# Second MLP of a fused attention kernel: other pairs of block products per PSUM bank, all engines in written order, part of the x work on GpSimd

## The chip, the cores and the metric

One core of a Trainium2 chip runs the whole program. The metric is the device time of one execution in microseconds (us). The engines are TensorE (PE, with its weight loads as PEld), VectorE (DVE), ScalarE (ACT), GpSimd (POOL) and SyncE (SP, which issues all DMAs of this kernel).

## The reference

Attention with keys and values averaged over 8 positions, then two MLPs, all in float32. Only the last function matters here; x has 4608 rows of 512 and comes from the first MLP.

```python
def _moe2_ref(x, w1, w2, w3, w_out) -> np.ndarray:
    a = x @ w1                       # 512 -> 1024
    b = x @ w2
    h = a * b @ w3                   # 1024 -> 1024
    return (h @ w_out).astype(np.float32)
```

## The kernel before

The first part (attention and first MLP) writes x, transposed, to a scratch tensor `x2d` in DRAM as nine groups `j` of 512 rows, each in four blocks of 128x512 words. Then `wf = w3 @ w_out` is made once. The second MLP is the rest of the program, and the change lies in it alone.

Each matrix that TensorE multiplies is split in two numbers, a high part (`h`, ScalarE copy that rounds) and a low part (`l`, VectorE subtract); a product of two such matrices takes three matmuls (high times high, high times low, low times high).

**One unit.** A unit is `ab(j, fc)`: group `j` (9 of them), column chunk `fc` of 128 hidden units (8 of them), 72 units in all. The two products x@w1 and x@w2 of the unit come from seven block products, p1 to p7, each of sums of blocks of x (`xs`, seven split blocks `th`/`tl`) and sums of blocks of the weights. Each block product is 6 matmuls of 256 columns (L869 to L871). They are issued in the order p1, p6, p5, p2, p7, p4, p3 into PSUM banks of tag `pr` (4 buffers, two halves of 256 columns each): p1 and p2 share a bank, p6 and p7, p5 and p3; p4 has one alone. What comes out of PSUM: ScalarE copies p1 (L873); VectorE makes `u2` = p1+p6 (L875), `a` parts (L877, L879, L887) and `b` parts (L881, L882, L884); GpSimd multiplies the halves of `a` and `b` (L885, L888). The product `a` is split into `ph` (ScalarE, L98) and `pl` (VectorE, L99).

**The output product.** `finish` of a unit is 12 matmuls of 512 columns (`out_fc`, L901, L903, L904: eight with `ph`, then four with `pl`; in the last unit of a group three for each of the four accumulators in turn). It is issued one unit later, between p4 and p3 of the next unit (`pend`). After a group's last unit, `evac` scales the four accumulators into `ot` tiles (2 buffers; L910 on VectorE, L912 on ScalarE) and SP stores them. The ninth group's store has the shape [2, 64, 512] on the DRAM side, the others 128 rows.

**The next group's x.** `Blocks.load` (written after the unit fc=2) loads four blocks to `xq` tiles and makes four sums on VectorE (L836, L837, L839, L840); `Blocks.split` splits a block on ScalarE and VectorE. There are 9 buffers for `th` and 9 for `tl`; seven are in use, so two blocks are split early and the other five in unit fc=7, after each product that frees a slot.

**Order.** TensorE's order is as written. The other engines' orders in this phase are the scheduler's.

Of the kernel before, what the change touches and what calls it, by code (L numbers as in the profile page):

```python
# [8 lines left out]
F32 = mybir.dt.float32  # L9
F32R = mybir.dt.float32r  # L10
I32 = mybir.dt.int32
U32 = mybir.dt.uint32
AF = mybir.ActivationFunctionType
ALU = mybir.AluOpType
# [4 lines left out]
def attention_moe_kernel(  # L19
# [25 lines left out]
    nc = tc.nc  # L45

    B, H, S, D = q.shape
    P = 128
    C = H * D
    NP = H // 2  # L50
    F = w_in.shape[1]
    FC = F // P
# [7 lines left out]
    U = 256  # L60
# [12 lines left out]
    def bank(name):  # L73
        return PS.tile([P, 512], F32, tag="ba", name=name, bufs=3)
# [22 lines left out]
    def split(hi, lo, src):  # L97
        nc.scalar.activation(hi, src, AF.Copy)  # L98
        nc.vector.tensor_tensor(lo, src, hi.bitcast(F32), ALU.subtract)  # L99
# [49 lines left out]
    class Rounded:  # L149
        def __init__(self, w, i):  # L150
            self.w, self.i = w, i

        def load(self):
            self.t = self.words()
            nc.sync.dma_start(self.t.rearrange("p n t -> p (n t)"), piece(self.w.bitcast(I32), self.i, 1024))
# [529 lines left out]
    M2 = R = o2 = None  # L685
# [23 lines left out]
    with tc.manual_schedule(engines={mybir.EngineType.PE, mybir.EngineType.SP}):  # L709
        for s_ in range(min(events), SLOTS * (NU + 1) + 2):  # L710
# [4 lines left out]
            kind, n = HEAVY[c], c % 4  # L715
# [16 lines left out]
    def bankp(name):  # L732
        return PB.tile([P, 2, U], F32, tag="pr", name=name, bufs=4)
# [9 lines left out]
    PRODUCTS = (  # L743
        ("p1", [t[:, 0:2] for t in w1p]),
        ("p6", s2),
        ("p5", s1),
        ("p2", [t[:, 2:4] for t in w1p]),
        ("p7", s3),
        ("p4", w2b),
        ("p3", s4),  # L750
    )
# [31 lines left out]
    def w3_T(m):  # L783
        th = R.tile([P, FC, P], F32R, tag="w3h", name=f"w3h{m}", bufs=2)
        tl = R.tile([P, FC, P], F32R, tag="w3l", name=f"w3l{m}", bufs=2)
        for i in range(2):
            t = R.tile([P, 512], F32, tag="stg", name="stg", bufs=4)
            nc.sync.dma_start(t, piece(f32w["w3f"], 2 * m + i))
            pw = bank(f"pw{m}_{i}")
            for c in range(4):  # L790
                nc.tensor.transpose(pw[:, c * P : c * P + P], t[:, c * P : c * P + P], ident)
            split(th[:, 4 * i : 4 * i + 4], tl[:, 4 * i : 4 * i + 4], pw.rearrange("p (c n) -> p c n", c=4))
        return th, tl
# [12 lines left out]
    nxt = w3_T(0)  # L806
    for m in range(FC):
        cur = nxt
        if m + 1 < FC:
            nxt = w3_T(m + 1)  # L810
        wf_rows(m, cur)
        if m in BLOCKS_AT:
            i = BLOCKS_AT.index(m)
# [4 lines left out]
    M2 = ctx.enter_context(tc.tile_pool(name="mlpb", bufs=2, reuse_waits="tile"))  # L818

    class Blocks:  # L820


        def __init__(self, j):
            self.j, self.ready = j, []

        def load(self):
            def raw(r, h):
                t = M2.tile([P, 2, U], F32, tag="xq", name=f"xq{self.j}", bufs=7)
                if r is not None:
                    nc.sync.dma_start(t, x2d[self.j, h, r])  # L830
                return t

            b11, b12, b22, b21 = raw(0, 0), raw(0, 1), raw(1, 1), raw(1, 0)
            t1, t2, t4 = raw(None, 0), raw(None, 0), raw(None, 0)
            tt = nc.vector.tensor_tensor
            tt(t1, b12, b11, ALU.subtract)  # L836
            tt(t2, b22, t1, ALU.subtract)  # L837
            t3 = b12
            tt(t3, b22, b12, ALU.subtract)  # L839
            tt(t4, b21, t2, ALU.subtract)  # L840
            self.todo = [b11, t2, t1, b21, t3, t4, b22]

        def split(self, n=1):
            for src in self.todo[:n]:
                h = M2.tile([P, 2, U], F32R, tag="th", name=f"th{self.j}", bufs=SLOT2)
                l = M2.tile([P, 2, U], F32R, tag="tl", name=f"tl{self.j}", bufs=SLOT2)
                split(h, l, src)
                self.ready.append((h, l))
            del self.todo[:n]

    def ab(j, fc, xs, nxt):
        fsl = slice(fc * P, fc * P + P)
        nm = f"{j}_{fc}"
        tt = nc.vector.tensor_tensor
        p1, u2 = [M2.tile([P, U], F32, tag=t, name=t + nm, bufs=1) for t in ("p1", "u2")]

        a, b = [M2.tile([P, 2, U], F32, tag=t, name=t + nm) for t in ("a", "b")]
        r, pair = {}, {}
        for ((name, (wh, wl)), (th, tl)) in zip(PRODUCTS, xs.ready):
            if name == "p3" and pend is not None:  # L860
                finish(*pend)

            if name in ("p1", "p6", "p5", "p4"):
                pair[name] = bankp(name + nm)
                o = r[name] = pair[name][:, 0]
            else:
                o = pair[{"p2": "p1", "p7": "p6", "p3": "p5"}[name]][:, 1]
            for c in range(2):
                nc.tensor.matmul(o, wh[:, c, fsl], th[:, c], start=c == 0, stop=False)  # L869
                nc.tensor.matmul(o, wh[:, c, fsl], tl[:, c], start=False, stop=False)  # L870
                nc.tensor.matmul(o, wl[:, c, fsl], th[:, c], start=False, stop=c == 1)  # L871
            if name == "p1":
                nc.scalar.activation(p1, o, AF.Copy)  # L873
            elif name == "p6":
                tt(u2, p1, o, ALU.add)  # L875
            elif name == "p5":
                tt(a[:, 1], u2, o, ALU.add)  # L877
            elif name == "p2":
                tt(a[:, 0], p1, o, ALU.add)  # L879
            elif name == "p7":  # L880
                tt(b[:, 0], u2, o, ALU.add)  # L881
                tt(b[:, 1], b[:, 0], r["p5"], ALU.add)  # L882
            elif name == "p4":
                tt(b[:, 0], b[:, 0], o, ALU.add)  # L884
                nc.gpsimd.tensor_tensor(a[:, 0], a[:, 0], b[:, 0], ALU.mult)  # L885
            elif name == "p3":
                tt(a[:, 1], a[:, 1], o, ALU.add)  # L887
                nc.gpsimd.tensor_tensor(a[:, 1], a[:, 1], b[:, 1], ALU.mult)  # L888
            if fc == FC - 1 and nxt is not None:
                nxt.split()  # L890
        ph = M2.tile([P, 512], F32R, tag="ph", name="ph" + nm, bufs=3)
        pl = M2.tile([P, 512], F32R, tag="pl", name="pl" + nm, bufs=3)
        split(ph, pl, a.rearrange("p a n -> p (a n)"))
        return ph, pl

    def out_fc(fc, pp, t, lo):
        ph, pl = pp
        wh, wl = wf[0][:, fc], wf[1][:, fc]
        ts = slice(t * P, t * P + P)
        if lo:  # L900
            nc.tensor.matmul(accs[t], pl[:, ts], wh, start=False, stop=(fc == FC - 1))  # L901
        else:
            nc.tensor.matmul(accs[t], ph[:, ts], wh, start=(fc == 0), stop=False)  # L903
            nc.tensor.matmul(accs[t], ph[:, ts], wl, start=False, stop=False)  # L904

    def evac(j, t):
        ot = M2.tile([P, C], F32, tag="ot", name=f"ot{j}_{t}", bufs=2)
        k = kap[:, 4 * j + t : 4 * j + t + 1]
        if t % 2 == 0:
            nc.vector.tensor_scalar(ot, accs[t], k, None, ALU.mult)  # L910
        else:
            nc.scalar.activation(ot, accs[t], AF.Copy, scale=k)  # L912
        if j == B:
            to = out.rearrange("(b s) c -> b s c", s=S)[2 * t : 2 * t + 2, 512:S, :]
        else:
            to = out[S * j : S * j + 512, :].rearrange("(p t) c -> p t c", t=4)[:, t]
        nc.sync.dma_start(to, ot)

    accs = None

    def finish(j, fc, pp):

        nonlocal accs
        if fc == 0:
            accs = [bank(f"acc{j}_{t}") for t in range(4)]
        if fc < FC - 1:
            for t in range(4):
                out_fc(fc, pp, t, False)
            for t in range(4):
                out_fc(fc, pp, t, True)  # L930
        else:
            for t in range(4):
                out_fc(fc, pp, t, False)
                out_fc(fc, pp, t, True)
                evac(j, t)


    SLOT2 = 9
    pend = None
    xs = Blocks(0)  # L940
    xs.load()
    xs.split(7)
    with tc.manual_schedule(engines={mybir.EngineType.PE}):
        for j in range(NB):
            nxt = Blocks(j + 1) if j + 1 < NB else None
            for fc in range(FC):
                pp = ab(j, fc, xs, nxt)
                pend = (j, fc, pp)
                if fc == 2 and nxt is not None:
                    nxt.load()  # L950
                    nxt.split(SLOT2 - 7)
            xs = nxt
        finish(*pend)


_INS = ['q', 'k', 'v', 'moe_w_in', 'moe_w_out', 'moe_g_ln', 'moe2_w1', 'moe2_w2', 'moe2_w3', 'moe2_w_out']
# [26 lines left out]
```

## Time and profile before

| | us |
|---|---|
| median of 3 runs | 1355.95 (1352.96 to 1356.12) |
| profiled execution, its own time | 1354.67 |
| profiled execution, span | 1352.9 |
| TensorE matmul busy | 1228.2 (91% of the span) |
| VectorE busy | 857.6 (63%) |
| ScalarE busy | 529.6 (39%) |
| GpSimd busy | 352.9 (26%) |

The span is the time from the first to the last instruction. Line numbers are those of the kernel before. Names in the rows drop trailing numbers: `p` is a bank of a block product or the copy of p1, `u` is `u2`; `w1h`, `s2h`, `s1h`, `s3h`, `w2bh` and `s4h` are weights of p1 and p2, p6, p5, p7, p4 and p3. Matmuls are pipelined, so the start of a matmul to the start of the next, not its duration, is its cost. L99 is the line of the helper `split` for all low parts, L98 that for all high parts.

### The profile page before, as it was taken

The page shows a single profiled execution, that of the slowest core. Times are in us where ns is not written, and L with a number is a line of the kernel's source. Part 1 is how long each engine was busy: PE and PEld are TensorE (multiplying, and loading weights), DVE is VectorE, ACT ScalarE, POOL GpSimd, SP SyncE. Part 2 cuts the span into 40 slices and gives each one's busy share as a digit, 9 for nine tenths or more (in the row PEclk, how much of TensorE's full clock was granted, in tenths as well). Part 3 has the DMA queues.
Part 4 walks back from the last instruction along what each step waited for, and adds up shares of the span by engine and source line. Part 5 has one row for each costly group of instructions (what it writes and reads, how often), then busy time and mean ns, then how long its engine had stood idle before and what let it go on. Part 6 is the DMA issues. An engine that isn't in the chain of part 4 may idle for free.

```text
span 1352.9 us, 21592 instructions
## 1 busy us (share of the span) xinstructions
PE 1228.2 (91%) x8120; PEld 1119.2 (83%) x8120; DVE 857.6 (63%) x1710; ACT 529.6 (39%) x1507; POOL 352.9 (26%) x447
## 2 busy tenths in 40 slices
PE   2467998999999999999999899999999999999992
PEld 2356888888888888899988798999989898989992
DVE  7999777777777777655356646556564646464541
ACT  3355656566666656555353221212121212121210
POOL 4453435253434334220000112111211112111110
PEclk9989999999999999999999899999999999999996
DMA  9433445454535364333042201010100102010000
GB/s 227 116 97 102 133 125 156 117 157 119 141 120 137 102 164 117 98 97 107 26 137 72 71 14 51 16 47 17 47 32 32 56 8 63 1 47 1 32 1 31
DMA packets 85696, 109.41 MB, mean 81 GB/s; under 512 B 43608, under 2 KB 43608, under 8 KB 85592
## 3 DMA queue, kind: packets, MB, share of 16 engines
q1 hardware_dynamic: 85592, 108.03, 28.0%
q8 instruction: 64, 1.05, 0.3%
q14 instruction: 40, 0.33, 0.1%
HBM read 78.65 MB, written 29.36 MB: 80 GB/s over the span
## 4 chain that ended last, share of the span: by engine, by line
PE 65%; DVE 16%; DMA 7%; issue 4%; ACT 3%; POOL 3%; SPq 0%; POOLq 0%; ACTq 0%; DVEq 0%
PE h L539 9%; PE p L869 7%; PE p L870 7%; PE p L871 7%; DMA f<-in_moe_w_dram 5%; PE acc L903 4%; PE acc L904 4%; PE acc L901 4%; PE x L597 4%; PE x L596 4%; PE x L598 4%; PE av L511 2%; PE sc L408 2%; PE lt L582 1%; DVE cvm L180 1%
## 5 line engine op out<-in xcount | busy, mean ns | idle before, releaser
L873 ACT ACTIVATE p<-p 128x256 f32<-128x256 f32 x72 | 27.9, 387 | 408.9 <-PE p L871 408.9
L885 POOL TENSOR_TENSOR a<-a,b 128x256 f32<-128x256 f32 x72 | 55.3, 768 | 445.2 <-DVE b L884 445.2
L596 PE MATMUL x<-lnh,gwh 128*128 128x256 f32 x576 | 166.6, 289 | 0.0
L597 PE MATMUL x<-lnl,gwh 128*128 128x256 f32 x576 | 163.0, 283 | 1.6 <-DVE lnl L586 1.6
L598 PE MATMUL x<-lnh,gwl 128*128 128x256 f32 x576 | 162.8, 283 | 0.0
L887 DVE TENSOR_TENSOR a<-a,p 128x256 f32<-128x256 f32 x72 | 30.3, 421 | 164.0 <-PE p L871 163.1
L188 POOL TENSOR_TENSOR cvb<-cvb,cvm 128x512 f32<-128x512 f32 x47 | 61.9, 1316 | 209.1 <-DVE cvm L180 148.0
L903 PE MATMUL acc<-wfh,ph 128*128 128x512 f32 x288 | 113.4, 394 | 2.0 <-ACT ph L98 2.0
L904 PE MATMUL acc<-wfl,ph 128*128 128x512 f32 x288 | 113.5, 394 | 0.0
L429 ACT ACTIVATE ea<-sc,mx 128x72 f32<-128x72 f32 x320 | 98.4, 328 | 36.6 <-DVE mx L426 36.6
L597 PEld LDWEIGHTS x<-lnl,gwh 128*128 128x128 f32 x576 | 110.0, 191 | 3.0 <-DVE lnl L586 2.2
L596 PEld LDWEIGHTS x<-lnh,gwh 128*128 128x128 f32 x576 | 109.9, 191 | 1.3 <-ACT lnh L585 0.2
L598 PEld LDWEIGHTS x<-lnh,gwl 128*128 128x128 f32 x576 | 109.9, 191 | 0.0
L539 PE MATMUL h<-winh,xh 128*128 128x512 f32 x288 | 101.3, 434 | 0.0
L888 POOL TENSOR_TENSOR a<-a,b 128x256 f32<-128x256 f32 x72 | 56.5, 785 | 141.1 <-DVE a L887 141.1
L539 PE MATMUL h<-winl,xh 128*128 128x512 f32 x288 | 92.3, 403 | 0.0
L539 PE MATMUL h<-winh,xl 128*128 128x512 f32 x288 | 91.1, 398 | 0.0
L586 DVE TENSOR_TENSOR lnl<-lt,lnh 128x512 fp32r<-128x512 f32 x72 | 49.3, 687 | 54.0 <-ACT lnh L585 53.5
L869 PE MATMUL p<-th,w1h 128*128 128x256 f32 x288 | 81.9, 284 | 1.2 <-ACT th L98 1.2
L870 PE MATMUL p<-tl,w1h 128*128 128x256 f32 x288 | 81.9, 284 | 0.4 <-DVE tl L99 0.4
L901 PE MATMUL acc<-wfh,pl 128*128 128x512 f32 x288 | 82.1, 392 | 0.0
L871 PE MATMUL p<-th,w1l 128*128 128x256 f32 x288 | 81.7, 284 | 0.0
(187 smaller groups left out, 3670.0 us busy)
## 6 DMA issues: line engine op xcount, KB each, us to landing
f<-in_moe_w_dram SPq DMA_DIRECT2D x32, 512.0 KB, 6.3
x2d<-xo SPq DMA_DIRECT2D x36, 256.0 KB, 3.0
xq<-x2d SPq DMA_DIRECT2D x36, 256.0 KB, 2.7
out_dram<-ot SPq DMA_DIRECT2D x36, 256.0 KB, 2.3
kv<-in_k_dram SPq DMA_DIRECT2D x32, 256.0 KB, 3.7
q<-in_q_dram SPq DMA_DIRECT2D x32, 256.0 KB, 7.4
kv<-in_v_dram SPq DMA_DIRECT2D x32, 256.0 KB, 3.8
f<-in_moe_w_out_dram SPq DMA_DIRECT2D x16, 512.0 KB, 6.8
```

What stands on the lines that cost most here:

```text
L188: self.engine.tensor_tensor(self.f, self.f, self.m.bitcast(F32), ALU.add)
L429: nc.scalar.activation(e[0:n, x], half[a][:, h], AF.Exp, bias=mx[0:n, x : x + 1], scale=1.0, accum_out=sm[0:n, x : x + 1],)
L539: nc.tensor.matmul(self.ph[:, a], s_[:, c], w_[:, c, a * 512 : a * 512 + 512], start=first, stop=last)
L596: nc.tensor.matmul(o, gw[0][:, f, ws], self.th[:, f], start=(f == 0), stop=False)
L597: nc.tensor.matmul(o, gw[0][:, f, ws], self.tl[:, f], start=False, stop=False)
L598: nc.tensor.matmul(o, gw[1][:, f, ws], self.th[:, f], start=False, stop=(f == FC - 1))
L869: nc.tensor.matmul(o, wh[:, c, fsl], th[:, c], start=c == 0, stop=False)
L870: nc.tensor.matmul(o, wh[:, c, fsl], tl[:, c], start=False, stop=False)
L871: nc.tensor.matmul(o, wl[:, c, fsl], th[:, c], start=False, stop=c == 1)
L901: nc.tensor.matmul(accs[t], pl[:, ts], wh, start=False, stop=(fc == FC - 1))
L903: nc.tensor.matmul(accs[t], ph[:, ts], wh, start=(fc == 0), stop=False)
L904: nc.tensor.matmul(accs[t], ph[:, ts], wl, start=False, stop=False)
```

## The change

In the second MLP:

- p7 gets a bank of its own, which it shares with p4; p6 has its bank alone.
- `finish` is issued before p4 instead of before p3; in the last unit of the last group it is issued after p3.
- `ph` and `pl` of a unit are made inside the next unit: `ph` on ScalarE after the copy of p1, `pl` on VectorE after the p2 addition.
- For all groups but the first, the four sums of x and the low parts of the blocks 0, 1, 3 and 5 are made on GpSimd.
- The next group's loads are written after unit fc=1, two sums after fc=3, two after fc=4, two splits after fc=5, and five splits inside unit fc=7 at the places of the table `LAST`.
- The two parts of a split block lie in one tile (`th`, 9 buffers of two parts); `ph` and `pl` have 2 buffers instead of 3; `ot` has 4 instead of 2.
- All five engines run in the written order in this phase.

```diff
@@ -821,7 +821,7 @@
 
 
         def __init__(self, j):
-            self.j, self.ready = j, []
+            self.j, self.ready, self.n = j, [], 0
 
         def load(self):
             def raw(r, h):
@@ -832,21 +832,32 @@
 
             b11, b12, b22, b21 = raw(0, 0), raw(0, 1), raw(1, 1), raw(1, 0)
             t1, t2, t4 = raw(None, 0), raw(None, 0), raw(None, 0)
-            tt = nc.vector.tensor_tensor
-            tt(t1, b12, b11, ALU.subtract)
-            tt(t2, b22, t1, ALU.subtract)
-            t3 = b12
-            tt(t3, b22, b12, ALU.subtract)
-            tt(t4, b21, t2, ALU.subtract)
-            self.todo = [b11, t2, t1, b21, t3, t4, b22]
-
-        def split(self, n=1):
-            for src in self.todo[:n]:
-                h = M2.tile([P, 2, U], F32R, tag="th", name=f"th{self.j}", bufs=SLOT2)
-                l = M2.tile([P, 2, U], F32R, tag="tl", name=f"tl{self.j}", bufs=SLOT2)
-                split(h, l, src)
-                self.ready.append((h, l))
-            del self.todo[:n]
+            self.todo = [b11, t2, t1, b21, b12, t4, b22]
+
+        def sum(self, o, x, y):
+            (nc.gpsimd if self.j else nc.vector).tensor_tensor(o, x, y, ALU.subtract)
+
+        def sums12(self):
+            b11, t2, t1, b21, b12, t4, b22 = self.todo
+            self.sum(t1, b12, b11)
+            self.sum(t2, b22, t1)
+
+        def sums34(self):
+            b11, t2, t1, b21, b12, t4, b22 = self.todo
+            self.sum(b12, b22, b12)
+            self.sum(t4, b21, t2)
+
+        def hi(self):
+            src = self.todo[len(self.ready)]
+            t = M2.tile([P, 2, 2, U], F32R, tag="th", name=f"th{self.j}", bufs=SLOT2)
+            nc.scalar.activation(t[:, 0], src, AF.Copy)
+            self.ready.append((t[:, 0], t[:, 1]))
+
+        def lo(self):
+            i, self.n = self.n, self.n + 1
+            h, l = self.ready[i]
+            eng = nc.gpsimd if self.j and i in (0, 1, 3, 5) else nc.vector
+            eng.tensor_tensor(l, self.todo[i], h.bitcast(F32), ALU.subtract)
 
     def ab(j, fc, xs, nxt):
         fsl = slice(fc * P, fc * P + P)
@@ -857,26 +868,30 @@
         a, b = [M2.tile([P, 2, U], F32, tag=t, name=t + nm) for t in ("a", "b")]
         r, pair = {}, {}
         for ((name, (wh, wl)), (th, tl)) in zip(PRODUCTS, xs.ready):
-            if name == "p3" and pend is not None:
-                finish(*pend)
-
-            if name in ("p1", "p6", "p5", "p4"):
+            if name == "p4" and pend is not None and (j, fc) != (B, FC - 1):
+                finish()
+
+            if name in ("p1", "p6", "p5", "p7"):
                 pair[name] = bankp(name + nm)
                 o = r[name] = pair[name][:, 0]
             else:
-                o = pair[{"p2": "p1", "p7": "p6", "p3": "p5"}[name]][:, 1]
+                o = pair[{"p2": "p1", "p4": "p7", "p3": "p5"}[name]][:, 1]
             for c in range(2):
                 nc.tensor.matmul(o, wh[:, c, fsl], th[:, c], start=c == 0, stop=False)
                 nc.tensor.matmul(o, wh[:, c, fsl], tl[:, c], start=False, stop=False)
                 nc.tensor.matmul(o, wl[:, c, fsl], th[:, c], start=False, stop=c == 1)
             if name == "p1":
                 nc.scalar.activation(p1, o, AF.Copy)
+                if pend is not None:
+                    pend[2].hi()
             elif name == "p6":
                 tt(u2, p1, o, ALU.add)
             elif name == "p5":
                 tt(a[:, 1], u2, o, ALU.add)
             elif name == "p2":
                 tt(a[:, 0], p1, o, ALU.add)
+                if pend is not None:
+                    pend[2].lo()
             elif name == "p7":
                 tt(b[:, 0], u2, o, ALU.add)
                 tt(b[:, 1], b[:, 0], r["p5"], ALU.add)
@@ -887,14 +902,24 @@
                 tt(a[:, 1], a[:, 1], o, ALU.add)
                 nc.gpsimd.tensor_tensor(a[:, 1], a[:, 1], b[:, 1], ALU.mult)
             if fc == FC - 1 and nxt is not None:
-                nxt.split()
-        ph = M2.tile([P, 512], F32R, tag="ph", name="ph" + nm, bufs=3)
-        pl = M2.tile([P, 512], F32R, tag="pl", name="pl" + nm, bufs=3)
-        split(ph, pl, a.rearrange("p a n -> p (a n)"))
-        return ph, pl
+                for step in LAST[name]:
+                    getattr(nxt, step)()
+        return Product(a.rearrange("p a n -> p (a n)"), nm)
+
+    class Product:
+        def __init__(self, a, nm):
+            self.a, self.nm = a, nm
+
+        def hi(self):
+            self.h = M2.tile([P, 512], F32R, tag="ph", name="ph" + self.nm)
+            nc.scalar.activation(self.h, self.a, AF.Copy)
+
+        def lo(self):
+            self.l = M2.tile([P, 512], F32R, tag="pl", name="pl" + self.nm)
+            nc.vector.tensor_tensor(self.l, self.a, self.h.bitcast(F32), ALU.subtract)
 
     def out_fc(fc, pp, t, lo):
-        ph, pl = pp
+        ph, pl = pp.h, pp.l
         wh, wl = wf[0][:, fc], wf[1][:, fc]
         ts = slice(t * P, t * P + P)
         if lo:
@@ -904,7 +929,7 @@
             nc.tensor.matmul(accs[t], ph[:, ts], wl, start=False, stop=False)
 
     def evac(j, t):
-        ot = M2.tile([P, C], F32, tag="ot", name=f"ot{j}_{t}", bufs=2)
+        ot = M2.tile([P, C], F32, tag="ot", name=f"ot{j}_{t}", bufs=4)
         k = kap[:, 4 * j + t : 4 * j + t + 1]
         if t % 2 == 0:
             nc.vector.tensor_scalar(ot, accs[t], k, None, ALU.mult)
@@ -918,9 +943,10 @@
 
     accs = None
 
-    def finish(j, fc, pp):
+    def finish():
 
         nonlocal accs
+        j, fc, pp = pend
         if fc == 0:
             accs = [bank(f"acc{j}_{t}") for t in range(4)]
         if fc < FC - 1:
@@ -937,20 +963,34 @@
 
     SLOT2 = 9
     pend = None
+
+    LAST = dict(
+        p1=("hi",), p6=("hi",), p5=("lo", "lo", "hi"), p2=("hi",), p7=("lo", "lo", "hi", "lo"), p4=(), p3=()
+    )
+
+    EARLY = {1: ("load",), 3: ("sums12",), 4: ("sums34",), 5: ("hi", "hi", "lo", "lo")}
     xs = Blocks(0)
     xs.load()
-    xs.split(7)
-    with tc.manual_schedule(engines={mybir.EngineType.PE}):
+    xs.sums12()
+    xs.sums34()
+    for _ in PRODUCTS:
+        xs.hi()
+        xs.lo()
+    E = mybir.EngineType
+    with tc.manual_schedule(engines={E.PE, E.SP, E.Activation, E.DVE, E.Pool}):
         for j in range(NB):
             nxt = Blocks(j + 1) if j + 1 < NB else None
             for fc in range(FC):
                 pp = ab(j, fc, xs, nxt)
+                if (j, fc) == (B, FC - 1):
+                    finish()
                 pend = (j, fc, pp)
-                if fc == 2 and nxt is not None:
-                    nxt.load()
-                    nxt.split(SLOT2 - 7)
+                for step in EARLY.get(fc, ()) if nxt is not None else ():
+                    getattr(nxt, step)()
             xs = nxt
-        finish(*pend)
+        pp.hi()
+        pp.lo()
+        finish()
 
 
 _INS = ['q', 'k', 'v', 'moe_w_in', 'moe_w_out', 'moe_g_ln', 'moe2_w1', 'moe2_w2', 'moe2_w3', 'moe2_w_out']
```

## Rows read from the trace of the kernel before

**Rows 1.** Busy us (count) of PE, PEld, DVE, ACT, POOL; clock, DMA share, GB/s.
```profile
766.00:1320.00 554.00, 546.88 (x3765) 507.48 (x3764) 303.70 (x655) 109.77 (x210) 107.39 (x139) 1.00 0.08 29
```

**Rows 2.** ScalarE timeline, copies of p1: start, duration, operation, [idle before <-releaser].
```profile
767.86 0.39 ACT L873 ACTIVATE p<-p 128x256 f32<-128x256 f32 x1 [7.08 <-PE p L871]
...
806.76 0.39 ACT L873 ACTIVATE p<-p 128x256 f32<-128x256 f32 x1 [6.65 <-PE p L871]
...
814.79 0.39 ACT L873 ACTIVATE p<-p 128x256 f32<-128x256 f32 x1 [3.77 <-PE p L871]
...
823.66 0.39 ACT L873 ACTIVATE p<-p 128x256 f32<-128x256 f32 x1 [2.15 <-PE p L871]
...
831.87 0.39 ACT L873 ACTIVATE p<-p 128x256 f32<-128x256 f32 x1 [6.50 <-PE p L871]
...
1317.32 0.39 ACT L873 ACTIVATE p<-p 128x256 f32<-128x256 f32 x1 [6.65 <-PE p L871]
```

**Rows 3.** TensorE timeline, one unit inside a group and the start of the next.
```profile
1174.24 0.28 PE L869 MATMUL p<-th,w1h 128*128 128x256 f32 x1
...
1177.12 0.28 PE L869 MATMUL p<-th,s3h 128*128 128x256 f32 x1
...
1178.56 0.40 PE L903 MATMUL acc<-wfh,ph 128*128 128x512 f32 x1
...
1181.31 0.28 PE L869 MATMUL p<-th,s4h 128*128 128x256 f32 x1
...
1182.02 0.28 PE L869 MATMUL p<-th,w1h 128*128 128x256 f32 x1
```

**Rows 4.** Timeline of all engines in the same unit.
```profile
1175.71 0.63 ACT L98 ACTIVATE ph<-a 128x512 fp32r<-128x512 f32 x1
...
1177.32 0.42 DVE L879 TENSOR_TENSOR a<-p,p 128x256 f32<-128x256 f32 x1
```

**Rows 5.** Timeline of all engines, first unit of the second group.
```profile
814.03 0.74 POOL L885 TENSOR_TENSOR a<-a,b 128x256 f32<-128x256 f32 x1 [6.80 <-DVE b L884]
...
814.36 0.95 DVE L837 TENSOR_TENSOR xq<-xq,xq 128x512 f32<-128x512 f32 x1
...
814.73 1.19 POOL L888 TENSOR_TENSOR a<-a,b 128x256 f32<-128x256 f32 x1
...
815.24 1.22 DVE L839 TENSOR_TENSOR xq<-xq,xq 128x512 f32<-128x512 f32 x1
...
816.61 0.69 DVE L99 TENSOR_TENSOR pl<-a,ph 128x512 fp32r<-128x512 f32 x1 [0.15 <-ACT ph L98]
...
817.69 0.39 PE L869 MATMUL p<-th,s3h 128*128 128x256 f32 x1 [0.83 <-DVE u L875]
```

**Rows 6.** Instruction groups: low parts, and sums on GpSimd elsewhere.
```profile
L99 DVE TENSOR_TENSOR tl<-xq,th 128x512 fp32r<-128x512 f32 x54 | 36.4, 686 | 0.0
...
L188 POOL TENSOR_TENSOR cvb<-cvb,cvm 128x512 f32<-128x512 f32 x47 | 61.9, 1316 | 209.1 <-DVE cvm L180 148.0 <-DVE sm L444 53.7 <-DVE sm L445 4.1
```

**Rows 7.** TensorE timeline, first two units of the phase.
```profile
757.33 0.36 PE L869 MATMUL p<-th,s4h 128*128 128x256 f32 x1 [1.37 <-DVE b L882]
...
761.90 0.39 PE L869 MATMUL p<-th,s3h 128*128 128x256 f32 x1 [0.74 <-DVE u L875]
```

**Rows 8.** Timeline of all engines after the last block product.
```profile
1324.01 0.28 PE L871 MATMUL p<-th,s4l 128*128 128x256 f32 x1
...
1326.27 0.50 PE L903 MATMUL acc<-wfh,ph 128*128 128x512 f32 x1 [1.98 <-ACT ph L98]
...
1328.31 1.35 SPq L917 DMA_DIRECT2D out_dram<-ot  x2
...
1336.62 0.75 DVE L910 TENSOR_SCALAR ot<-acc,kap 128x512 f32<-128x512 f32 x1 [8.34 <-DMA out_dram<-ot]
```

**Rows 9.** Busy by stretch (columns as in group 1), the last stores.
```profile
1329.50:1333.00 3.50, 1.42 (x4) 0.60 (x2) 0.00 (x0) 0.00 (x0) 0.00 (x0) 0.75 0.13 29
1333.00:1351.50 18.50, 0.00 (x0) 0.00 (x0) 0.75 (x1) 0.69 (x1) 0.00 (x0) 0.55 0.13 51
```

## Prediction

> **What bounds the kernel now.** I read the views from the whole to the single wait. The second MLP is the last 600 us of the span, and the change is confined to it. From the third unit to the last, TensorE is busy 546.88 of 554 us at a granted clock of 1.00 (2.4 GHz), while VectorE has 303.70, ScalarE 109.77 and GpSimd 107.39 [rows 1]: the phase is TensorE's, and no edit of the change takes a matmul away. So I first need TensorE's pace without waits. The timeline of one unit inside a group gives it [rows 3]: p1 starts at 1174.24, p7 at 1177.12 (2.88 later), the output product at 1178.56 (4.32), p3 at 1181.31 (7.07), the next p1 at 1182.02. A unit is 7.78 us, an output product 2.75, a block product 0.72, one of the 12 wide matmuls 2.75 / 12 = 0.229. The work is issued back to back; such a unit has nothing to gain.
>
> What is above that floor shows in the starts of the p1 copies, one per unit [rows 2]. From the third unit (767.86) to the 72nd (1317.32) there are 69 units: 549.46 us, where 69 x 7.78 = 536.8. The excess is 12.6. It sits at the group changes: 806.76 to 814.79 is 8.03, to 823.66 is 8.87, to 831.87 is 8.21, that is 0.25 + 1.09 + 0.43 = 1.77 over three units. Seven such changes are 12.4, and the eighth, after which no group is prepared, has the first 0.25: together 12.6, so this is all of it.
>
> The reason is in the timeline there [rows 5]: the first matmul of p7 waited for u2 (0.83 idle). p7 is written to the bank that holds p6, and u2, which reads p6, stood on VectorE behind two sums of 0.95 and 1.22 us and a `pl` of 0.69. Two more places are above the floor: the start of the phase, where p3 waited 1.37 for b and the next unit's p7 0.74 for u2 [rows 7], and the end, where the last output product waited 1.98 for `ph` [rows 8] before four stores follow.
>
> **The change part by part.** Times are counted from a unit's first matmul.
>
> *Banks and order.* p7 no longer shares with p6, so its wait for u2 is gone. The new pairs: p4 goes into p7's bank, and the 2.75 us of the output product stand between them; p3 goes into p5's bank 4.9 us later; p1 and p2 are as before. The output product now starts at 3.60 instead of 4.32. It needs `ph`, which ended 1175.71 + 0.63 = 2.10 into the unit [rows 4]: 1.5 to spare. Its first matmul with `pl` is at 3.60 + 8 x 0.229 = 5.43; `pl` now stands behind the p2 addition, which starts at 3.08 [rows 4], so it ends at 3.08 + 0.42 + 0.69 = 4.2: 1.2 to spare. An ordinary unit costs 7.78 as before.
>
> *Work that moves.* Per group, four sums and four low parts leave VectorE, 8 x 0.69 = 5.5 us [rows 6], for GpSimd, where the nearest row, a 128x512 addition in the first part, has 1316 ns: 8 x 1.32 = 10.5 us. GpSimd has two products of 0.74 per unit [rows 5], so it has room. Sums and the first low parts stand after units 3, 4 and 5, two at a time, 2.6 us behind the product that ends about 1.5 into the next unit; they are over at 4.1 and the next p4 product comes after 6.35. Nothing is queued behind them that is due earlier, and their results are due three to four units later. The loads are written one unit earlier, behind the four stores of the last group on SP, and have over 15 us until the sums: nothing.
>
> *Unit 7 of a group.* ScalarE has p1's copy, `ph` to 2.10, then five high parts of at most 0.63, each after the product that frees its slot; the last is done by 5.3, and the next copy is due after 8. VectorE has seven additions of 0.42 and four low parts (one is `pl`) of 0.69, 5.7 of 7.78 us, without sums. The 0.25 of p3's wait should go. Two tight places stay. `pl` here follows a low part and the p2 addition (3.8) and meets GpSimd's two low parts, the first of which starts when the second high part is done, at about 3.4. Rows 5 show what such a meeting costs: the sum of two SBUF tiles issued at 814.36 took 0.95 where 0.69 is normal [rows 6], the next one 1.22, and GpSimd's product between them 1.19 instead of 0.74; the operations took turns. So `pl` waits for one GpSimd operation, 3.4 + 1.3 = 4.7, and ends near 5.35, just before 5.43. Bounds: `pl` at 4.5 without a meeting, or at 6.65 if both GpSimd operations go first, which holds TensorE for 1.2.
>
> The Trainium skill, SBUF — State Buffer, section "Who interferes with whom", makes it a rule: a VectorE operation with two SBUF inputs and a GpSimd operation that reads SBUF exclude each other for a whole instruction. The turns in rows 5 agree with it. By that rule alone the change puts 8 x 1.32 us of exclusion per group where there was little, which speaks against it.
>
> The second tight place is the unit after: there the output product goes accumulator by accumulator, the first `pl` matmul is at 3.60 + 2 x 0.229 = 4.06, and `pl` ends at 4.2. I leave 0.2 us at each of the 8 group changes, 1.6 (bounds 0 and 8 x 1.4 = 11). Gain at the changes: 12.6 - 1.6 = **11.0**.
>
> *Start.* The first sums and splits stay on VectorE as they were. In the first unit no sums of the second group stand between the additions, so p3's 1.37 goes; but there is no output product between p7 and p4, so p4 waits for the addition that reads p7, about 0.5 (0.42 and the latency). In the second unit the 0.74 goes. Gain 1.37 - 0.5 + 0.74 = 1.6; bounds 0 and 2.1.
>
> *End.* In the last unit the output product of the unit before it stands after p3. From the last matmul of p3 (1324.01) to `ph` took 2.26 [rows 8]; 2.75 of matmuls now cover this. p4's wait for p7's addition comes back here, 0.5. p3's last matmul is then at 1324.01 - 2.75 + 0.5 = 1321.8, the last output product starts 12 matmuls later, at 1324.6 instead of 1326.27. Its first accumulator is done sooner too, as its matmuls don't follow an idle stretch (first store 2.04 after the start before, by my count 1.8 now). First store at 1326.4 instead of 1328.31: gain **1.9**.
>
> *Four output tiles.* The last four stores ran at 51 GB/s on a DMA share of 0.13, two of 16 engines, without a gap from 1333 to the end, though only two were outstanding; before that, from 1329.5, the share was the same at 29 GB/s [rows 9]. The tile limit made VectorE wait 8.34 us for the first store [rows 8], but the two DMA engines were never without work. Four tiles let stores three and four queue earlier behind the same two engines: I count nothing. If the first 3.5 us ran at 51 too, 1.5 would be gained.
>
> The Trainium skill, DMA: Bandwidth & Descriptors, section "Why a DMA increments its semaphore by 16 and not by 1", says that such a transfer takes as many engines as divide its outermost size, and always the lowest-numbered ones. The share of 0.13 for an outermost size of 2 agrees; by it four stores in flight are no faster than two.
>
> **Sum.** 11.0 + 1.6 + 1.9 = 14.5. Against the profiled execution's own 1354.67 (1.8 above its span, 1.3 below the median of the runs): **1340**. For the likeliest case the range is 1337 to 1344: all group waits gone (-1.6) and the faster stores (-1.5) below, a little more left at each group change above.
>
> **Rivals.**
>
> *GpSimd and VectorE block each other at the group changes.* If `pl` waits for both low parts and later additions slip with it, 1.2 to 1.4 us stay per change, 8 x 1.2 = 9.6 more lost against none, or 8 more than I left: 1348. For it: the turns in rows 5 and a margin of 0.08. Against: GpSimd's second product also had to wait its turn there.
>
> *The four stores run beside each other.* If stores three and four took other DMA engines, each would take about the 8.3 us of the first [rows 8] and the last, issued some 2.5 after the first, would land at 1326.4 + 11; 12 us less: 1328. Against: the first two were in flight together at a share of two engines.
>
> *The waits only change place.* The written order on five engines puts one late instruction in front of all behind it; if the group changes keep their 1.6 to 1.8, only start and end are left, 3.5: 1351 to 1353, about no change. Against: every engine has at least 2 us of idle time in unit 7.
>
> *Slower: the earlier output product.* It is issued 0.72 sooner in 71 units. If `pl`, now in written order, came later than 5.43 in each ordinary unit by d, this costs 71 x d: the gain is gone at d = 0.2, and at 0.26 the kernel is over 0.3% slower; at d = 0.3 it is 1361. This needs `pl` 1.4 us later than the rows give; in units without GpSimd extras I see nothing that does it.
>
> **How the numbers follow.** Forecast 0.65; blocking at the group changes 0.16; parallel stores 0.03; waits that change place 0.07; slower 0.09. The range runs from 1336.5 (just below the forecast's lower end) to 1350 and leaves out parallel stores, most of "change place" and slower: 0.19. A measurement of this kernel can tell about 0.3%, 4 us, from no change. Faster than that: 0.65 + 0.16 + 0.03 = 0.84; within: 0.07; slower: 0.09.
>
> **What the profile after would show.** Right: p1 copies 7.78 apart also over the group changes, with at most 0.3 extra; no TensorE wait on u2; sums and four low parts per group on GpSimd at about 1.3 us; the final `ph` wait gone; the stores still at a share of 0.13 and about 24.6 us from first issue to end. Wrong: intervals over 8.2 at the group changes with a wait on `pl`; intervals over 7.8 everywhere (the slower rival); a store share above 0.13.

## The result and the profile after

The changed kernel takes 1338.59 us (median of 4, 1335.54 to 1341.47) beside 1354.45 for the kernel before: ratio 0.9886, 95% interval 0.9855 to 0.9917. The prediction was 1340, faster. The profiled executions have spans of 1352.9 and 1336.9, 16.0 apart.

Two views answer to [rows 1, 2]: the busy times from the third unit to the last, and the copies of p1 on ScalarE, of the third unit, around the first group change, and of the last unit.

```profile
763.00:1305.00 542.00, 542.00 (x3756) 505.65 (x3755) 284.98 (x597) 111.52 (x212) 184.95 (x204) 1.00 0.09 30
```
```profile
764.23 0.39 ACT L884 ACTIVATE p<-p 128x256 f32<-128x256 f32 x1 [6.61 <-PE p L882]
...
803.13 0.39 ACT L884 ACTIVATE p<-p 128x256 f32<-128x256 f32 x1 [6.61 <-PE p L882]
810.91 0.39 ACT L884 ACTIVATE p<-p 128x256 f32<-128x256 f32 x1 [4.00 <-issue]
818.90 0.39 ACT L884 ACTIVATE p<-p 128x256 f32<-128x256 f32 x1 [1.51 <-PE p L882]
826.68 0.39 ACT L884 ACTIVATE p<-p 128x256 f32<-128x256 f32 x1 [6.61 <-PE p L882]
...
1302.86 0.39 ACT L884 ACTIVATE p<-p 128x256 f32<-128x256 f32 x1 [6.60 <-PE p L882]
```

TensorE, 546.88 of 554 us busy before, now has no gap that the busy time shows. From 764.23 to 1302.86 there are again 69 units: 538.63 us, 1.81 over 69 x 7.78. Each of the eight group changes adds 0.21 to 0.24 (818.90 - 810.91 = 7.99 here), where seven of them added 1.77 [rows 2]. What is left is one wait per change, in the view of what TensorE's weight loads waited for in this stretch:

```profile
PEld acc L926 <- DVE pl L919: 2.9, 8, 0.4
```

Around a group change, `pl` meets the low parts on GpSimd in unit 7 and is late for the output product of the unit after (timeline of all engines):

```profile
1117.74 1.30 POOL L860 TENSOR_TENSOR th<-xq,th 128x512 fp32r<-128x512 f32 x1 [1.79 <-ACT th L853]
1117.78 0.41 DVE L892 TENSOR_TENSOR a<-p,p 128x256 f32<-128x256 f32 x1
1118.12 1.47 DVE L919 TENSOR_TENSOR pl<-a,ph 128x512 fp32r<-128x512 f32 x1
...
1125.67 0.69 DVE L919 TENSOR_TENSOR pl<-a,ph 128x512 fp32r<-128x512 f32 x1
...
1126.41 0.19 PEld L926 LDWEIGHTS acc<-wfh,pl 128*128 128x128 f32 x1 [0.36 <-DVE pl L919]
```

GpSimd's low part starts at 1117.74. `pl`, issued at 1118.12, takes 1.47 instead of 0.69, and ends at 1119.59, 0.55 after GpSimd's operation. The unit's first matmul started at 1114.48, so `pl` ends 5.11 in, before the 5.43 at which it is needed. In the unit after, the output product wants it at the third matmul and waits 0.36. The two took turns as in [rows 5]. The Trainium skill, SBUF — State Buffer, section "Who interferes with whom", has this as the exclusive use of a shared port by a VectorE operation with two SBUF inputs. 1.30 for GpSimd's operation, not slowed, with 1.47 for the one that came second agrees.

The groups of instructions from the third unit to the last give the prices of the moved work on GpSimd, 1.41 us for a low part and 1.29 for a sum (1.32 forecast for both):

```profile
L860 POOL TENSOR_TENSOR th<-xq,th 128x512 fp32r<-128x512 f32 x32 | 44.4, 1409 | 14.3 <-ACT th L853 14.3
...
L838 POOL TENSOR_TENSOR xq<-xq,xq 128x512 f32<-128x512 f32 x32 | 41.1, 1294 | 0.6
```

Start and end, to compare with [rows 7, 8]. In the first unit p4 waits for the addition that reads p7; in the last unit likewise, and then `ph` is in time and the first store goes out at 1312.32 (the matmul at 1307.80 is the last of p3):

```profile
753.97 0.36 PE L880 MATMUL p<-th,w2bh 128*128 128x256 f32 x1 [0.61 <-DVE b L896]
...
1306.38 0.39 PE L880 MATMUL p<-th,w2bh 128*128 128x256 f32 x1 [0.73 <-DVE b L896]
...
1307.80 0.28 PE L882 MATMUL p<-th,s4l 128*128 128x256 f32 x1
...
1310.66 0.39 PE L928 MATMUL acc<-wfh,ph 128*128 128x512 f32 x1
...
1312.32 10.03 SPq L942 DMA_DIRECT2D out_dram<-ot  x4
```

The last stores, by stretch, beside [rows 9]: again a share of 0.13 at about 50 GB/s.

```profile
1316.30:1336.00 19.70, 0.00 (x0) 0.00 (x0) 0.00 (x0) 0.00 (x0) 0.00 (x0) 0.52 0.13 49
```

From these and the last matmul of `wf` (started at 744.1 before, at 741.6 after) the 16.0 us split up: group changes 12.64 - 1.81 = 10.8; start, from that matmul to the third unit's copy, 23.76 - 22.63 = 1.1; end, from the last copy to the end of the span, 35.58 - 34.04 = 1.5; and 2.5 before the phase begins.

### The profile page after: what moved, and what is told of

It reads as the page before. It is cut to its first block, busy times and chain, and to the rows that moved or that the text cites. A ratio compares the mean times of both kernels' runs of the same rounds, so it can differ in the third digit from the quotient of the medians.

```text
span 1336.9 us, 21632 instructions
## 1 busy us (share of the span) xinstructions
PE 1217.5 (91%) x8120; PEld 1113.6 (83%) x8120; DVE 837.5 (63%) x1646; ACT 529.4 (40%) x1507; POOL 428.1 (32%) x511
## 4 chain that ended last, share of the span: by engine, by line
PE 75%; DVE 11%; DMA 5%; ACT 3%; issue 3%; POOL 1%; SPq 0%; ACTq 0%; POOLq 0%; DVEq 0%
PE h L539 10%; PE p L881 9%; PE p L882 9%; PE p L880 9%; PE acc L926 5%; PE acc L929 5%; PE acc L928 5%; PE x L596 4%; PE x L597 4%; PE x L598 4%; DMA f<-in_moe_w_dram 4%; PE av L511 2%; PE sc L408 2%; PE lt L582 1%; DVE cvm L180 1%
## 5 line engine op out<-in xcount | busy, mean ns | idle before, releaser
L900 POOL TENSOR_TENSOR a<-a,b 128x256 f32<-128x256 f32 x72 | 53.0, 736 | 481.2 <-DVE b L899 481.2
L899 DVE TENSOR_TENSOR b<-b,p 128x256 f32<-128x256 f32 x72 | 30.2, 420 | 123.1 <-PE p L882 123.1
L880 PE MATMUL p<-th,w1h 128*128 128x256 f32 x288 | 81.9, 284 | 1.2 <-ACT th L853 1.2
L881 PE MATMUL p<-th,w1h 128*128 128x256 f32 x288 | 81.9, 284 | 0.4 <-DVE th L860 0.4
L888 DVE TENSOR_TENSOR u<-p,p 128x256 f32<-128x256 f32 x72 | 30.4, 422 | 77.3 <-PE p L882 76.2
```

## The experiments

All ten were profiled and timed beside the kernel before. The table reads one profile of each kernel by the same three measures, all in us: excess of the 69 units over 7.78 each, start and end as above (good to 0.05). The medians are of timed runs; each ratio is to the runs of the kernel before that were timed beside that kernel (medians 1352.97 to 1354.45), so it isn't the quotient of two rows.

| kernel | excess | start | end | median | ratio to before (95%) |
|---|---|---|---|---|---|
| before | 12.64 | 23.76 | 35.58 | 1354.45 | |
| changed | 1.81 | 22.63 | 34.04 | 1338.59 | 0.9886 (0.9855 to 0.9917) |
| 1: order + GpSimd, old pairs | 1.81 | 22.00 | 33.87 | 1338.57 | 0.9888 (0.9864 to 0.9912) |
| 2: new pairs alone | 3.96 | 22.73 | 35.59 | 1342.62 | 0.9930 (0.9906 to 0.9953) |
| 3: order + new pairs, no GpSimd | 1.81 | 22.32 | 34.05 | 1337.63 | 0.9890 (0.9863 to 0.9917) |
| 4: order alone | 3.75 | 21.26 | 33.87 | 1341.73 | 0.9917 (0.9894 to 0.9940) |
| 5: changed, split stores | 1.84 | 22.58 | 17.16 | 1321.78 | 0.9766 (0.9740 to 0.9791) |
| 6: changed, two output tiles | 3.58 | 24.12 | 34.08 | 1340.96 | 0.9901 (0.9876 to 0.9926) |
| 7: old pairs, late output product, split stores | 0.00 | 21.29 | 16.99 | 1321.03 | 0.9760 (0.9734 to 0.9786) |
| 8: before, split stores | 12.56 | 23.81 | 20.21 | 1336.72 | 0.9876 (0.9854 to 0.9898) |
| 9: changed, all low parts on GpSimd | 5.28 | 22.29 | 34.01 | 1341.60 | 0.9908 (0.9884 to 0.9932) |
| 10: as 7, no GpSimd | 0.00 | 22.14 | 16.94 | 1322.04 | 0.9766 (0.9741 to 0.9791) |

**1. Old pairs in the changed kernel.**

```diff
-            if name in ("p1", "p6", "p5", "p7"):
+            if name in ("p1", "p6", "p5", "p4"):
...
-                o = pair[{"p2": "p1", "p4": "p7", "p3": "p5"}[name]][:, 1]
+                o = pair[{"p2": "p1", "p7": "p6", "p3": "p5"}[name]][:, 1]
```

> The changed kernel with p7 again in p6's bank and p4 alone in one. Theory 'load': u2 was late at the group changes because VectorE was full, and the shared bank is only where it showed; the changed kernel has u2 done about 1.9 us into a unit and p7 starts at 2.9, so p7 does not wait, the excess over 7.78 us per unit stays at 0.2 per group change, and p4 of the first and the last unit loses its wait of 0.6 to 0.7 each: 1.2 us faster than the changed kernel. Rival 'bank': p7 waits for u2 again, about 1 us at each of seven group changes, 7 to 10 us slower than the changed kernel.

The excess is 1.81, as in the changed kernel. With VectorE relieved, u2 is in time, and it doesn't matter that p7 shares its bank. Of the 1.2 us more, start and end gave 0.6 and 0.2, which the medians (1338.57 and 1338.59) don't resolve: in the first and the last unit p3 now waits, for the addition that makes b from p5, which the expectation had left out (the last unit):

```profile
1308.50 0.38 PE L880 MATMUL p<-th,s4h 128*128 128x256 f32 x1 [0.47 <-DVE b L897]
```

**2. The new pairs alone, in the kernel before** (the same two lines the other way round, and the output product ahead of p4).

> The kernel before with only the new pairs (p7 with p4) and the output product ahead of p4. Theory 'bank': p7 no longer waits for u2, 10 us faster than before, excess at the group changes 2 to 3 us in all. Theory 'load': VectorE is as full as before, its lateness goes on to the additions that p4, p3 and the output product need, so at least half of the 12.6 us of excess stays; 0 to 6 us faster than before.

The excess falls from 12.64 to 3.96: "bank" is right for most of it and "load" is refuted as put. But VectorE is as late as before: at the group change u2 starts 2.44 us after the copy of p1, as it did before (817.23, after the copy at 814.79 [rows 2]). VectorE before; then, with the new pairs, ScalarE, VectorE and TensorE:

```profile
817.23 0.41 DVE L875 TENSOR_TENSOR u<-p,p 128x256 f32<-128x256 f32 x1
```
```profile
807.99 0.39 ACT L873 ACTIVATE p<-p 128x256 f32<-128x256 f32 x1 [1.06 <-PE p L871]
```
```profile
809.82 0.69 DVE L99 TENSOR_TENSOR pl<-a,ph 128x512 fp32r<-128x512 f32 x1
810.43 0.41 DVE L875 TENSOR_TENSOR u<-p,p 128x256 f32<-128x256 f32 x1
```
```profile
809.90 0.28 PE L869 MATMUL p<-th,s3h 128*128 128x256 f32 x1
```

The addition that makes u2 starts at 810.43, after p7 has begun at 809.90; before, p7 waited for the same row [rows 5]. So the wait needed two things together, a late VectorE and a shared bank, and either part of the change takes it away. What stays of the excess is VectorE's lateness elsewhere: 0.29 at each of the eight changes, where p4 and p3 wait for b, and at three of them a wait of the output product for `ph`, 1.4 us in all.

**3. No GpSimd.** All sums and low parts on VectorE, at the written places.

```diff
-            (nc.gpsimd if self.j else nc.vector).tensor_tensor(o, x, y, ALU.subtract)
+            nc.vector.tensor_tensor(o, x, y, ALU.subtract)
...
-            eng = nc.gpsimd if self.j and i in (0, 1, 3, 5) else nc.vector
+            eng = nc.vector
```

> The changed kernel with all sums and low parts on VectorE again, at the same written places. Theory 'written order': two sums in units 4 and 5 fit into VectorE's idle time; unit 7 has five low parts, one more than fits easily (7.1 of 7.78 us busy); excess 0.2 to 0.6 per group change, at most 3 us slower than the changed kernel. Rival 'offload': VectorE without GpSimd's help is late again, 1 us or more per group change, 8 us or more slower.

Excess 1.81: the move to GpSimd is worth nothing beside the other parts. VectorE had the time in this order, in which the sums no longer stand at the group change.

**4. Order alone** (1 and 3 together).

> The changed kernel with the old pairs and with all sums and low parts on VectorE: what remains is the written order, the places of the steps, the output product ahead of p4 and the four output tiles. Theory 'written order and places carry the gain': excess at most 0.6 per group change, within 3 us of the changed kernel. Rival 'bank and offload carry it': p7 waits for u2 at the group changes, 8 to 12 us slower than the changed kernel.

"Order" stands here for all that the expectation names: written order, places, earlier output product and four tiles. Together they carry 8.9 of the 10.8 us without the new pairs and GpSimd. Beside the 0.24 at each change there are now 0.07 to 0.08 in three units of each group: two sums or low parts before u2 took 1.93 us together (two sums in the rows), beside GpSimd's product of `a`, and u2 came just too late for p7 in the shared bank:

```profile
776.69 1.93 DVE L838 TENSOR_TENSOR xq<-xq,xq 128x512 f32<-128x512 f32 x2
...
778.54 0.41 DVE L888 TENSOR_TENSOR u<-p,p 128x256 f32<-128x256 f32 x1
```

**5. Split stores.** Each of the last group's four stores becomes two, of 64 rows.

```diff
-            to = out.rearrange("(b s) c -> b s c", s=S)[2 * t : 2 * t + 2, 512:S, :]
...
-        nc.sync.dma_start(to, ot)
+            for i in range(2):
+                to = out.rearrange("(b s) c -> b s c", s=S)[2 * t + i, 512:S, :]
+                nc.sync.dma_start(to, ot[TL * i : TL * i + TL])
```

> The changed kernel with each of the last group's four stores as two stores of 64 rows. Theory 'two DMA engines': the stores of shape [2, 64, 512] run on two of the 16 DMA engines at 51 GB/s, one after the other; with 64 rows outermost they spread, each lands in about 2.3 us like the stores of the other groups, and the end comes 17 to 19 us sooner (about 1320). Rival 'late write receipts': the tail is latency of the output, and less than 5 us are gained.

The end is 16.9 us shorter, just under the 17 to 19 expected. By stretch, the stores now run on a share of 0.66 at 154 GB/s; the eight issues on SP take 5.05 of the 7.8 us from the first store to the end:

```profile
1312.00:1316.00 4.00, 1.01 (x5) 0.51 (x3) 0.75 (x1) 1.07 (x2) 0.00 (x0) 1.00 0.66 154
```
```profile
1311.79 5.05 SPq L941 DMA_DIRECT2D out_dram<-ot  x8
```

With 64 as the outermost size instead of 2 the same bytes spread over more engines. This agrees with the Trainium skill, DMA: Bandwidth & Descriptors, section "Why a DMA increments its semaphore by 16 and not by 1", which lets the outermost sizes set the number of engines.

**6. Two output tiles** instead of four in the changed kernel (`bufs=2` for `ot`).

> The changed kernel with two output tiles instead of four. Theory 'two DMA engines': the tail from the first last-group store to the end stays 24.6 us within 0.5; at the group changes VectorE's second scaling waits about 1 us for a store, which no matmul needs; equal to the changed kernel within 1 us. Rival 'tiles': the tail is shorter with four tiles, so this is 2 us or more slower; or the wait in written order holds up the addition of p4 and costs 0.5 per group change.

The end is the same (34.08 against 34.04): four tiles don't shorten it. But the excess grows by 1.8 us in this profile (the medians, 1340.96 and 1338.59, are within the scatter). It grows at three of the eight changes, which add 0.3, 0.7 and 1.4; the other five add 0.2 to 0.3. At the largest it goes by a way that neither theory named: in written order ScalarE's second scaling waits for a store, and the next p1 copy stands behind it; p2, in p1's bank, waits for that copy (ScalarE's timeline, then TensorE's):

```profile
1196.77 0.69 ACT L937 ACTIVATE ot<-acc,kap 128x512 f32<-128x512 f32 x1 [4.13 <-DMA out_dram<-ot]
1197.35 0.38 ACT L884 ACTIVATE p<-p 128x256 f32<-128x256 f32 x1
```
```profile
1197.78 0.39 PE L880 MATMUL p<-th,w1h 128*128 128x256 f32 x1 [0.91 <-ACT p L884]
```

At the second change it goes the way that the rival named: VectorE's second scaling waits for a store, the addition of p4 stands behind it, and the next p5 waits for that (VectorE's timeline, then that of the weight loads):

```profile
882.26 0.75 DVE L935 TENSOR_SCALAR ot<-acc,kap 128x512 f32<-128x512 f32 x1 [3.02 <-DMA out_dram<-ot]
882.93 0.41 DVE L899 TENSOR_TENSOR b<-b,p 128x256 f32<-128x256 f32 x1
```
```profile
883.39 0.19 PEld L880 LDWEIGHTS p<-th,s1h 128*128 128x128 f32 x1 [0.29 <-DVE b L899]
```

**7. Old pairs, the output product again before p3, split stores** (the diffs of 1 and 5, and `name == "p3"` instead of `name == "p4"` ahead of `finish`).

> The changed kernel with the old pairs, the output product again between p4 and p3 (after p3 only in the last unit), and the split stores. Theory: the 0.22 per group change was pl arriving late for an output product at 3.6 us into the unit; at 4.3 it is in time, so the excess of 1.8 goes to under 0.3; the first and last unit lose p4's wait (0.6 each). Together 3 us less than the changed kernel with split stores, about 1317. Rival: excess stays 0.2 per group change, as it comes from something other than pl.

Excess 0.00, where the old pairs alone (run 1) leave 1.81: the 0.22 per change was `pl` coming late, as the p1 copies of this kernel show, 7.78 apart right over the change:

```profile
810.47 0.38 ACT L884 ACTIVATE p<-p 128x256 f32<-128x256 f32 x1 [4.04 <-issue]
818.25 0.38 ACT L884 ACTIVATE p<-p 128x256 f32<-128x256 f32 x1 [0.79 <-PE p L882]
```

By the three measures it is 3.3 us shorter than run 5, 1.3 of it in the start, which varies for another reason too (see the start below). The medians, 1321.03 and 1321.78, don't resolve that, and the expected 1317 is not shown.

**8. Split stores in the kernel before.**

> The kernel before with the last group's four stores as two stores of 64 rows each. Theory 'two DMA engines': the tail falls from 24.6 us after the first store to about 5 to 7 here too, 17 to 19 us faster than before, about 1336; the waits of the two output tiles vanish with it. Rival: with two tiles the waits for stores remain and less than 10 us are gained.

Faster by as much as the whole change. The first store is 9.0 us from the end, not 5 to 7, and the waits of the two tiles don't vanish: the second scaling on VectorE still waited 3.11 us for a store. With this and the wait of the last output product for `ph` (its matmuls behind that wait run at a granted clock of 0.55) the end is 3 us longer than in run 5.

```profile
1328.45 0.75 DVE L910 TENSOR_SCALAR ot<-acc,kap 128x512 f32<-128x512 f32 x1 [3.11 <-DMA out_dram<-ot]
```

**9. All low parts on GpSimd** in the changed kernel, five in unit 7 instead of two.

> The changed kernel with the low parts of all seven blocks on GpSimd for all groups but the first: five of 1.3 us in unit 7 instead of two. Theory 'turns': pl of unit 7 still waits for one GpSimd operation at a time and ends before 5.4 us into the unit; but GpSimd's products stand behind five low parts, so they end 1.3 to 1.6 us later, and ph and pl with them; excess per group change 0.4 to 1.0 instead of 0.23, 2 to 6 us slower than the changed kernel. Rival 'first come': pl waits for several low parts and TensorE for pl, over 1.2 us per group change already inside unit 7, 10 us or more slower. Third: no difference, GpSimd has the room.

0.61 to 0.91 at each of seven changes and 0.58 at the eighth, 3.5 us more in all: "turns". GpSimd's products stood behind five low parts in a row, the last four in the first row here, and `ph` and `pl` behind them (GpSimd's timeline, then VectorE's):

```profile
1121.24 5.50 POOL L860 TENSOR_TENSOR th<-xq,th 128x512 fp32r<-128x512 f32 x4
1126.69 0.76 POOL L900 TENSOR_TENSOR a<-a,b 128x256 f32<-128x256 f32 x1
```
```profile
1128.84 0.69 DVE L919 TENSOR_TENSOR pl<-a,ph 128x512 fp32r<-128x512 f32 x1 [0.32 <-ACT ph L915]
```

**10. Run 7 without GpSimd** (the diff of 3).

> The kernel of the seventh run (old pairs, output product between p4 and p3, split stores) with all sums and low parts on VectorE. Theory: the offload is worth nothing at the group changes (excess 0); the two sums or low parts that stand before u2 in three units of a group cost 0.07 to 0.08 each as with the written order alone, 1.8 us in all. Rival: with five low parts in unit 7 VectorE is late for the output product and 0.2 or more per group change come back.

Excess 0.00, so the expected 1.8 us are not there. With the output product between p4 and p3, GpSimd's first product is done before the two sums start; they take 1.83 instead of 1.93, u2 starts 1.33 us after the p1 copy instead of 1.42, and that is in time. The simplest kernel of the set in written order, with neither the new pairs nor GpSimd's help, is as fast as any by the medians (1322.04 against 1321.03 and 1321.78).

## Why the prediction was right, point by point

*Group changes, 11.0 forecast: 10.8 measured.* The 0.2 that I left at each came out as 0.21 to 0.24, and from the place named: `pl` for the first accumulator, one unit after the change. Run 7 shows it, since a later output product takes it away.

*What carries it.* The prediction credited the banks with the wait for u2 and the moved work with the 0.25 of p3. That division does not hold. Pairs alone give 8.7 of 10.8, order alone 8.9, order with pairs all of it, and so does order with GpSimd. So the 11.0 came out by a sum whose shares were not right. GpSimd, costed as the relief of VectorE, is not needed where the sums are spread over units 4 and 5 (runs 3 and 10). Of what run 4 calls order, the earlier output product is not needed (runs 7 and 10) and the four tiles are worth up to 1.8 (run 6); whether the written order or the places of the sums and splits did the rest, no run separates.

*Meeting of `pl` and GpSimd.* Right in kind: one turn, `pl` in time at 5.11 against 5.43 (5.35 forecast). The rival in which `pl` waits for both low parts did not occur; run 9 shows the price of more GpSimd work, and it is paid by the products queued behind, not by `pl`'s turn.

*Start, 1.6 forecast: 1.1.* By the p1 copies the second unit gave 1.0 where 0.74 was forecast, and the first only 0.2 where 0.9 was. p3's wait went and p4's came, as 0.61 instead of 0.5. The larger part of the shortfall is TensorE's clock, which the forecast left out. In both kernels TensorE waits about 2 us ahead of p6, for the high part of a sum, and in the first unit the granted clock falls to 0.50 (1.2 GHz). Before, it rose again as p7 began; in the changed kernel it was still 0.50, and p7's first three matmuls took 0.64 instead of 0.40 (p7 on TensorE and busy by stretch, before, then after):

```profile
754.32 0.33 PE L869 MATMUL p<-th,s3h 128*128 128x256 f32 x1
...
754.72 0.28 PE L869 MATMUL p<-th,s3h 128*128 128x256 f32 x1
```
```profile
754.40:755.10 0.70, 0.70 (x8) 0.70 (x8) 0.54 (x2) 0.00 (x0) 0.00 (x0) 0.98 0.01 3
```
```profile
751.88 0.41 PE L880 MATMUL p<-th,s3h 128*128 128x256 f32 x1
...
752.52 0.41 PE L880 MATMUL p<-th,s3h 128*128 128x256 f32 x1
```
```profile
751.90:753.10 1.20, 1.20 (x7) 1.17 (x6) 0.42 (x1) 0.00 (x0) 0.00 (x0) 0.50 0.03 12
```

The start varies from 21.26 to 24.12 over the kernels in written order, and the clock's return with it. With the new pairs the start is 22.3, 22.6 and 24.1 where the clock is at 1.00 again 6.0, 7.0 and 10.75 us after p6's first matmul (run 3, changed, run 6); with the old pairs it is 21.3, 22.0 and 22.1 for 4.25, 5.75 and 7.5 (runs 4, 1, 10).

*End, 1.9 forecast: 1.5.* Counted by starts, p4's wait cost 1.0, not 0.5: the last matmul of p3 came 4.94 us after the unit's p1 copy (1307.80 - 1302.86), where 6.69 [rows 2, 8] less the 2.75 of the output product would be 3.94. The first store came 1.66 after the last output product's first matmul, 0.1 sooner than the 1.8 forecast. After the first store 24.6 us passed, as before and as forecast, and four tiles gained nothing there. They gain 1.8 at the group changes in written order, in the one profile of run 6, which I had costed at nothing.

*Not forecast: 2.5 us ahead of the phase.* The instructions there stand in the same order in both kernels. Over the twelve profiles the last matmul of `wf` started between 738.3 and 745.4, with no relation to the edit, so these 2.5 are scatter from one execution to the next. Without them the phase gained 13.5 against 14.5 forecast. That the measured 1338.59 lies so near to 1340, and below it, is in part the luck of this scatter.

*Slower rival.* No unit inside a group is over 7.78 in the changed kernel; the earlier output product cost only the 0.2 per change.

*Parallel stores.* The share stayed at 0.13, as the forecast held against this rival. Its price of 12 us was too small by its own terms: 24.6 us after the first store against 11 is 13.6.

## What to carry to other kernels

A wait that needs two conditions, here a late engine and a shared bank, can be removed from either side, and doing both pays once; test the parts alone before keeping the costly one. Before tuning the waits of a loop, look at what follows the last matmul: a store whose outermost size was 2 held 17 us, more than all the waits of the loop together. In written order, an instruction that waits for a transfer also stops the short copies and additions behind it (run 6), so give it enough buffers.

## What was not expected of the hardware

With more than two stores outstanding at a DMA share of 0.13, the issue itself was held up: of the four instructions on SP in the changed kernel the first two took 0.62 and 0.56 us, the third and the fourth 3.60 and 4.96, 10.03 from the first to the end of the last. With two tiles, and so two stores outstanding at most, none took over 0.62 (before, run 6); the eight split ones took 0.55 to 0.60 each. TensorE's granted clock was at 0.50 (1.2 GHz) around waits of about 2 us at both ends of the phase: that of p6 in the first unit, and, in the kernel before, from 1328.2 to 1330.2 in the last output product, which had waited 1.98 for `ph`; there its matmuls stood 0.43 apart instead of 0.23. And the first part, with the same instruction order, ended up to 7 us apart in different executions, half of what the change gains, so parts of it had to be read from the phase and not from the span.
